# Second pair's xt copies behind its state products, and a state update moved to the third pair, in a retention and bilinear-MLP kernel

## The chip, the cores and the metric

The kernel runs on one core of a Trainium2 chip. The metric is the device time of one execution in microseconds (us); lower is better. The core's engines work side by side, each through its own list of instructions: TensorE (PE, with its weight loads shown apart as PEld), VectorE (DVE), ScalarE (ACT), GpSimd (POOL) and SyncE (SP), which issues the transfers. [...]

## What is computed

A retention recurrence over 4 batches, 8 heads, 768 positions and 64 features per head, followed by a bilinear MLP on the 3072 tokens:

```python
for t in range(S):
    state = gamma[None, :, None, None] * state + np.einsum('bhd,bhe->bhde', k[:, :, t], v[:, :, t])
    y[:, :, t] = scale * np.einsum('bhd,bhde->bhe', q[:, :, t], state)
...
x = attn_out.transpose(0, 2, 1, 3).reshape(B * S, H * D)
return ((x @ w_a) * (x @ w_b)) @ w_out
```

with w_a and w_b of 512x1536 and w_out of 1536x512. The output is float32; the kernel multiplies in bfloat16 and accumulates in float32.

## The kernel before

**The recurrence in chunks.** The decay is folded into tables that scale k and q, so that what is left is causal attention without a softmax. Tokens go in 24 slots of 128. Within a chunk of 64 positions the output is the masked score matrix times v (the intra products); what comes from earlier chunks is q times a running state (the state products), where the state is the sum of k times v over those chunks.

**The first batch** is worked in three pairs of slots (`PAIRS = 3`), u = 0, 1, 2, by functions whose names end in 2. A pair is loaded with even and odd positions in its two slots (par 0 and 1), and its chunks are its two halves c = 0 and 1. For each pair the code calls, by hand and in a chosen order:
- `casts2`: scales k and q and casts v, on the engines named;
- `flip2(u, K or Q, ...)`: transposes of k or q on PE, 128x128 each, and copies out of PSUM to kT2 or qT2 (`L397`);
- `scores2` and `mask2`: score products (`L410`) and the causal mask on DVE (`L421`);
- `intra2(u, par, begin, home)`: 16 intra products (`L466`) for one slot of the pair. They write y, which with `home` given is one PSUM tile whose two halves are `ys[u][0]` and `ys[u][1]`; so it is for u = 1;
- `inter2(u, last, cs)`: eight state products (`L451`) for each c named. Those of c take the state gbd[c], and add to the same y;
- `update2(u, c, on)`: 16 products of 64x64 (`L434`) that add chunk c of the pair to the state sum `st`, which stays in PSUM, then `keep_state(c, on)`, two casts of `st` into gbd[1 - c] on the engines in `on`; with `on=None` no casts;
- `leave2(u, on)`: casts y half by half into xt, the transposed activations that the MLP reads (`L182` on ACT, `L184` on DVE).

**The MLP** goes over token blocks `TILES = [4, 2, 2, 2, 2, 4, 4, 4]` in slots. For block J and one of 12 feature groups ft, `ffn_a` makes four products with w_a over the 512 input features (`L510`), which ACT casts to bfloat16 as asb (`L514`), and `ffn_g` four with w_b (`L522`), which DVE multiplies with asb into ht (`L525`). `ffn_out` makes the output products (`L550`). The results of `ffn_a` and `ffn_g` share three PSUM buffers, `ff`. The first block's first two groups are done by column halves: columns 0 to 255 (`0, W2`) are pair 0, columns 256 to 511 (`W2, 2 * W2`) are pair 1.

**What sets the order.** Every instruction passes through `seq`, which ties it to the one before it on its engine, so each engine runs in the order of the source. Waits between engines are put in from the tiles that are read and written. The weights are cast from float32 by POOL (`cast_w`), in the order in which their transfers land; `issue_loads(100)` puts the rest of the loads on SP's queue. After pair 1, 12 feature groups of block 0 run, and pair 2 is worked in among its last ones: `flip2(2, K)`, `ffn_a(0, 9)`, `flip2(2, Q)`, `ffn_g(0, 9)`, scores and masks, `update2(2, 0)` and so on. `flip2(2, K)` and the second half of `flip2(2, Q)` use the same PSUM bank, y0.

The part of the order that the change touches, before:

```python
    inter2(1, False, (0,))
    intra2(1, 1, False)
    leave2(1, (A_, None))
    W2 = 2 * P
    ffn_a(0, 0, 0, W2)
    inter2(1, True, (1,))
    leave2(1, (None, D_))
    ffn_a(0, 1, 0, W2)
    update2(1, 1, None)
```

Of the kernel before, what the change touches and what calls it, by code (L numbers as in the profile page):

```python
# [23 lines left out]
def kernel(  # L24
# [46 lines left out]
    def seq(bi):  # L71
        ins = bi.ins
        prev = last.get(ins.engine)
        if prev is not None:
            tc.add_manual_dep(ins, prev.name, nosync, reason="program order")
        last[ins.engine] = ins
        return bi
# [36 lines left out]
    def issue_loads(n):  # L114
        for _ in range(min(n, len(pending))):
            what = pending.pop(0)
            if what[0] in "kqv":
                load_pair(what[0], int(what[1:]))
            else:
                {"s": load_slot, "w": load_w, "o": load_o}[what[0]](int(what[1:]))  # L120
# [59 lines left out]
    def cast(engine, dst, src):  # L180
        if engine is nc.scalar:
            seq(nc.scalar.copy(dst, src))  # L182
        else:
            seq(engine.tensor_copy(dst, src))  # L184
# [50 lines left out]
    def half(i):  # L235
        return slice(64 * i, 64 * i + 64)
# [151 lines left out]
    def flip2(u, i, on, banks=None):  # L388
        into = (kT2, qT2)[i]
        if u not in into:  # L390
            into[u] = tra.tile([P, 2, HP, P], BF16, tag="kq"[i] + "T2", name="kq"[i] + "T2", bufs=2)
        for pars, eng in on:
            pool, tag = (psff, "ff") if not banks or not banks[pars[0]] else (psat, banks[pars[0]])
            tp = pool.tile([P, 2, HP, P], BF16, tag=tag, name="tp")[:, : len(pars)]
            for m, par in enumerate(pars):
                for hp in range(HP):
                    seq(nc.tensor.transpose(tp[:, m, hp, :], kqb[2 * u + par][:, i, hp, :, :], ident))  # L397
            cast(eng, into[u][:, pars[0] : pars[0] + len(pars)], tp)
# [25 lines left out]
    def update2(u, c, on=(nc.scalar, nc.scalar)):  # L424
        if (u, c) == (PAIRS - 1, 1):
            return
        if (u, c) == (0, 0):
            state[0] = psst.tile([P, HP, D], F32, tag="st", name="st")
        st = state[0]
        for par in range(2):  # L430
            for hp in range(HP):
                for r in range(2):
                    t = 2 * u + par
                    seq(nc.tensor.matmul(st[half(r), hp, :], kb[t][half(c), hp, r, :],  # L434
                                         vb[t][half(c), HP * r + hp, :],
                                         start=((u, c, hp, par) == (0, 0, 0, 0)),
                                         stop=(hp == HP - 1), skip_group_check=True))
        if on:
            keep_state(c, on)

    def keep_state(c, on=(nc.scalar, nc.scalar)):
        for r in range(2):
            cast(on[r], gbd[1 - c][half(r), :, half(r)], state[0][half(r), :, :])

    def inter2(u, last=False, cs=(0, 1)):
        for c in cs:
            if (u, c) == (0, 0):
                continue
            for r in range(2):
                for hp in range(HP):  # L450
                    seq(nc.tensor.matmul(ys[u][c][half(hp % 2), 2 * r + hp // 2, :],  # L451
                                         gbd[c][:, hp, half(r)],
                                         qT2[u][:, :, hp, half(c)], start=False, stop=last,
                                         skip_group_check=True))

    def intra2(u, par, begin, home=None):
        if begin and home is None:
            ys[u] = [psat.tile([P, HP, P], F32, tag=f"y{c}", name="y") for c in range(2)]
        elif begin:
            both = psat.tile([P, 2, HP, P], F32, tag=home, name="y")  # L460
            ys[u] = [both[:, c] for c in range(2)]
        t = 2 * u + par
        for r in range(2):
            for hp in range(HP):
                for c in range(2):
                    seq(nc.tensor.matmul(ys[u][c][half(hp % 2), 2 * r + hp // 2, :],  # L466
                                         vb[t][half(c), HP * r + hp, :], aT[t][half(c), r, hp, :],
                                         start=(begin and r == 0 and hp < 2), stop=not begin,
                                         skip_group_check=True))

    def leave2(u, on):
        J, i = where[2 * u]
        if i == 0 and J not in xt:
            xt[J] = xtp.tile([P, 4, KT, P], BF16, tag="xt", name="xt")
        for c, eng in enumerate(on):
            if eng is None:
                continue
            cast(eng, xt[J][:, i + c].rearrange("p k (m par) -> p k par m", par=2),
                 ys[u][c].rearrange("p k (par m) -> p k par m", par=2))

    def xcols(J, kt, c0, c1):
        if J < 2:
            return xt[J][:, c0 // P : c1 // P, kt, :]
        return xt[J][:, kt, c0:c1]
# [11 lines left out]
    def parts(J, ft, c0, c1):  # L496

        if J == 0 and ft in (2, 3):
            return [(c0, (c0 + c1) // 2), ((c0 + c1) // 2, c1)]
        return [(c0, c1)]  # L500

    def ffn_a(J, ft, c0=0, c1=None):
        c1 = TILES[J] * P if c1 is None else c1
        if J not in ht:
            ht[J] = htp.tile([P, NFT, 4 * P], BF16, tag="ht", name="ht")
        fs = slice(ft * P, (ft + 1) * P)
        a = psff.tile([P, 4 * P], F32, tag="ff", name="a")[:, : c1 - c0]
        for kt in range(KT):
            for b0, b1 in parts(J, ft, c0, c1):
                seq(nc.tensor.matmul(a[:, b0 - c0 : b1 - c0], wa_bf[:, kt, fs], xcols(J, kt, b0, b1),  # L510
                                     start=(kt == 0 and b0 == c0), stop=(kt == KT - 1 and b1 == c1),
                                     skip_group_check=True))
        asb = asbs[J, ft, c0] = asbp.tile([P, 4 * P], BF16, tag="asb", name="asb")[:, : c1 - c0]
        seq(nc.scalar.copy(asb, a))  # L514

    def ffn_g(J, ft, c0=0, c1=None):
        c1 = TILES[J] * P if c1 is None else c1
        fs = slice(ft * P, (ft + 1) * P)
        g = psff.tile([P, 4 * P], F32, tag="ff", name="g")[:, : c1 - c0]
        for kt in range(KT):  # L520
            for b0, b1 in parts(J, ft, c0, c1):
                seq(nc.tensor.matmul(g[:, b0 - c0 : b1 - c0], wb_bf[:, kt, fs], xcols(J, kt, b0, b1),  # L522
                                     start=(kt == 0 and b0 == c0), stop=(kt == KT - 1 and b1 == c1),
                                     skip_group_check=True))
        seq(nc.vector.tensor_tensor(ht[J][:, ft, c0:c1], g, asbs.pop((J, ft, c0)), op=ALU.mult))  # L525

    def ffn_ab(J, ft):
        store()
        ffn_a(J, ft)
        ffn_g(J, ft)  # L530
        catch_up(2)
# [30 lines left out]
    D_, G_, A_ = nc.vector, nc.gpsimd, nc.scalar  # L562
# [36 lines left out]
    intra2(1, 0, True, "at")  # L599
    update2(1, 0, (D_, D_))  # L600
    inter2(1, False, (0,))
    intra2(1, 1, False)
    leave2(1, (A_, None))
    W2 = 2 * P
    ffn_a(0, 0, 0, W2)
    inter2(1, True, (1,))
    leave2(1, (None, D_))
    ffn_a(0, 1, 0, W2)
    update2(1, 1, None)
    issue_loads(100)  # L610
    cast_w(1)
    ffn_g(0, 0, 0, W2)
# [2 lines left out]
    ffn_g(0, 1, 0, W2)  # L615
    ffn_g(0, 0, W2, 2 * W2)
    ffn_g(0, 1, W2, 2 * W2)
    keep_state(1)
    for ft in range(2, NFT):
        if ft % FPW == 0 and ft // FPW + 1 < NW - 1:  # L620
            cast_w(ft // FPW + 1)
# [8 lines left out]
        if ft == 8:  # L630
            ffn_ab(0, ft)
    flip2(2, K, [((0, 1), A_)], ("y0", None))
    ffn_a(0, 9)
    flip2(2, Q, [((0,), D_), ((1,), D_)], ("y1", "y0"))
    ffn_g(0, 9)
# [80 lines left out]
```

## Time and profile before

| | us |
|---|---|
| median of 3 runs | 225.2 (225.17 to 225.49) |
| the profiled execution | 225.04 |
| its span, first to last instruction | 223.3 |
| PE busy | 217.2 |
| DVE busy | 98.0 |
| ACT busy | 94.3 |
| POOL busy | 79.5 |

The profile is of one execution. Its timeline gives for each instruction, or for a run of like ones (xN), the start in us from the span's start, the length in us, the engine, the line, the operation and the tiles as out<-in; in brackets stands how long the engine was idle just before, and what ended that. Matmuls overlap in the pipeline, so the length of a group holds the time until its last result is written, while the next group starts earlier. Line numbers that start with L are those of the kernel before; a line such as L182 or L184 is a helper's that casts on ACT or on DVE and POOL.

### The profile page before, as it was taken

How to read it: one execution, taken by the hardware profiler on the slowest of the kernel's cores; microseconds unless marked ns; L12 is line 12 of the kernel's file. 1: busy time of each engine (PE TensorE's matmuls, PEld its weight loads, DVE VectorE, ACT ScalarE, POOL GpSimd, SP SyncE). 2: the span in 40 equal slices, each digit the busy share in tenths (PEclk: the TensorE clock that was granted, in tenths of full speed). 3: DMA queues.
4: the chain of work that ended last, by engine and by line, in shares of the span. 5: the costliest groups of instructions: out<-in, count | busy, mean ns of one | idle time of the engine just before them, and what ended most of it. 6: DMA issues, size and time to landing. Idle time of an engine off the chain costs nothing.

```text
span 223.3 us, 6286 instructions
## 1 busy us (share of the span) xinstructions
PE 217.2 (97%) x2633; PEld 131.4 (59%) x2633; DVE 98.0 (44%) x202; ACT 94.3 (42%) x202; POOL 79.5 (36%) x104
## 2 busy tenths in 40 slices
PE   7799999999999999999999999999999999999994
PEld 7568555785457866876875444554444544444443
DVE  3784446643316436572476333533333521333300
ACT  3784335343425425453456333455333354333221
POOL 5557798682634435351622535350000000000000
PEclk9999999999999999999999999999999999999999
DMA  6999999998999997999989497974100012100022
GB/s 179 346 379 382 366 292 396 300 217 178 221 244 230 256 219 101 229 203 231 236 181 222 96 268 190 248 127 144 47 0 0 3 50 94 47 3 0 3 94 94
DMA packets 96124, 39.72 MB, mean 178 GB/s; under 512 B 76000, under 2 KB 91616, under 8 KB 96096
## 3 DMA queue, kind: packets, MB, share of 16 engines
q1 hardware_dynamic: 95952, 39.20, 68.2%
q8 instruction: 20, 0.33, 0.6%
q10 hardware_dynamic: 144, 0.13, 0.2%
q14 instruction: 8, 0.07, 0.1%
HBM read 28.31 MB, written 6.29 MB: 155 GB/s over the span
## 4 chain that ended last, share of the span: by engine, by line
PE 93%; DMA 3%; POOL 1%; SPq 0%; ACT 0%; issue 0%; POOLq 0%
PE o L550 28%; PE g L522 28%; PE a L510 28%; DMA kf<-in_k_dram 3%; PE y L322 1%; POOL kqb L212 1%; PE y L334 1%; PE at L281 1%; PE st L257 1%; PE y L451 1%; PE st L434 1%; PE y L466 1%; PE tp L397 1%; PE at L410 0%; SPq L95 0%; ACT xt L182 0%
## 5 line engine op out<-in xcount | busy, mean ns | idle before, releaser
L525 DVE TENSOR_TENSOR ht<-g,asb 128x256 bf16<-128x256 f32 (+1 forms) x98 | 53.9, 550 | 82.3 <-PE g L522 73.8
L510 PE MATMUL a<-xt,wa_bf 128*128 128x256 bf16 (+1 forms) x400 | 77.7, 319 | 0.0
L522 PE MATMUL g<-xt,wb_bf 128*128 128x256 bf16 (+1 forms) x400 | 77.7, 319 | 0.0
L514 ACT CAST asb<-a 128x256 bf16<-128x256 f32 (+1 forms) x98 | 46.3, 472 | 71.8 <-PE a L510 71.8
L550 PE MATMUL o<-wo_bf,ht 128*128 128x512 bf16 (+2 forms) x312 | 64.5, 363 | 0.0
L510 PEld LDWEIGHTS <-wa_bf 128*128 128x128 bf16 x400 | 38.8, 98 | 23.9 <-DVE xt L184 0.4
L522 PEld LDWEIGHTS <-wb_bf 128*128 128x128 bf16 x400 | 38.9, 98 | 23.0
L550 PEld LDWEIGHTS <-ht 128*128 128x128 bf16 x312 | 28.8, 98 | 30.5
L212 POOL TENSOR_TENSOR kqb<-kf,ktab 128x512 bf16<-128x512 f32 x21 | 22.3, 1065 | 37.7 <-DMA kf<-in_k_dram 30.0
L182 ACT COPY osb<-o 128x512 f32<-128x512 f32 (+2 forms) x25 | 14.1, 564 | 36.3 <-PE o L550 29.9
L212 POOL TENSOR_TENSOR kqb<-qf,qtab 128x512 bf16<-128x512 f32 x21 | 22.3, 1063 | 2.4 <-DMA qf<-in_q_dram 2.3
L184 POOL CAST vb<-vf 128x512 bf16<-128x512 f32 x24 | 14.4, 610 | 20.8 <-DMA vf<-in_v_dram 15.1
L271 DVE TENSOR_TENSOR sums<-st,sums 128x256 f32<-128x256 f32 x30 | 12.7, 424 | 1.6
L182 ACT CAST gst<-sums 128x256 bf16<-128x256 f32 x26 | 10.4, 406 | 5.1 <-DVE sums L271 2.4
L287 DVE TENSOR_TENSOR aT<-at,mask 128x512 bf16<-128x512 f32 x18 | 11.5, 679 | 0.0
L345 ACT CAST xt<-y 128x512 bf16<-128x512 f32 x16 | 8.5, 584 | 0.7 <-PE y L334 0.7
L489 PE MATMUL idle<-zero 128*128 128x170 bf16 (+4 forms) x57 | 6.5, 275 | 1.3 <-DVE zero L126 1.3
L421 DVE TENSOR_TENSOR aT<-at,mask 128x512 bf16<-128x512 f32 x12 | 7.4, 682 | 0.2 <-PE at L410 0.2
L184 POOL CAST wa_bf<-wsta 128x1024 bf16<-128x1024 f32 (+1 forms) x7 | 6.4, 918 | 3.1 <-DMA wsta<-in_moe_w_a_dram 3.1
L184 POOL CAST wo_bf<-wsto 128x1024 bf16<-128x1024 f32 x6 | 6.2, 1040 | 2.8 <-DMA wsto<-in_moe_w_out_dram 2.8
L184 POOL CAST wb_bf<-wstb 128x1024 bf16<-128x1024 f32 (+1 forms) x7 | 6.4, 919 | 1.4 <-DMA wstb<-in_moe_w_b_dram 1.1
L299 DVE COPY lgr<-bq 128x1 f32<-128x1 f32 x4 | 0.6, 154 | 13.8 <-PE y L322 13.8
(56 smaller groups left out, 94.6 us busy)
## 6 DMA issues: line engine op xcount, KB each, us to landing
out_dram<-osb SPq DMA_DIRECT2D x23, 256.0 KB, 2.8
kf<-in_k_dram SPq DMA_DIRECT2D x18, 256.0 KB, 3.8
qf<-in_q_dram SPq DMA_DIRECT2D x18, 256.0 KB, 4.3
vf<-in_v_dram SPq DMA_DIRECT2D x18, 256.0 KB, 5.2
wsta<-in_moe_w_a_dram SPq DMA_DIRECT2D x6, 512.0 KB, 7.6
wstb<-in_moe_w_b_dram SPq DMA_DIRECT2D x6, 512.0 KB, 7.9
wsto<-in_moe_w_out_dram SPq DMA_DIRECT2D x6, 512.0 KB, 9.9
kf<-in_k_dram SPq DMA_DIRECT2D x3, 512.0 KB, 5.8
```

Source lines behind the costliest of these rows:

```text
L182: seq(nc.scalar.copy(dst, src))
L184: seq(engine.tensor_copy(dst, src))
L212: seq(eng.tensor_tensor(dst, src, tab, op=ALU.mult))
L271: seq(nc.vector.tensor_tensor(new, u[c][:, s], old, op=ALU.add))
L287: seq(nc.vector.tensor_tensor(aT[n][:, r].rearrange("p s h d -> p (s h) d"), at[:, r].rearrange("p s h d -> p (s h) d"), mask.to_broadcast ...
L345: seq(nc.scalar.copy(dst, ys[o][c]))
L421: seq(nc.vector.tensor_tensor(aT[t][:, r], ats[t][r], masks[par].to_broadcast([P, HP, P]), op=ALU.mult))
L510: seq(nc.tensor.matmul(a[:, b0 - c0 : b1 - c0], wa_bf[:, kt, fs], xcols(J, kt, b0, b1), start=(kt == 0 and b0 == c0), stop=(kt == KT - 1 a ...
L514: seq(nc.scalar.copy(asb, a))
L522: seq(nc.tensor.matmul(g[:, b0 - c0 : b1 - c0], wb_bf[:, kt, fs], xcols(J, kt, b0, b1), start=(kt == 0 and b0 == c0), stop=(kt == KT - 1 a ...
L525: seq(nc.vector.tensor_tensor(ht[J][:, ft, c0:c1], g, asbs.pop((J, ft, c0)), op=ALU.mult))
L550: seq(nc.tensor.matmul(o, ht[J][:, ft, i * P : (i + 1) * P], wo_bf[:, ft, c0:c1], start=(ft == 0), stop=(ft == NFT - 1)))
```

## The change

```diff
     intra2(1, 0, True, "at")
     update2(1, 0, (D_, D_))
     inter2(1, False, (0,))
-    intra2(1, 1, False)
-    leave2(1, (A_, None))
     W2 = 2 * P
     ffn_a(0, 0, 0, W2)
+    intra2(1, 1, False)
     inter2(1, True, (1,))
-    leave2(1, (None, D_))
+    leave2(1, (A_, D_))
     ffn_a(0, 1, 0, W2)
-    update2(1, 1, None)
     issue_loads(100)
     cast_w(1)
     ffn_g(0, 0, 0, W2)
...
     ffn_g(0, 1, W2, 2 * W2)
-    keep_state(1)
     for ft in range(2, NFT):
...
     flip2(2, K, [((0, 1), A_)], ("y0", None))
+    update2(1, 1)
     ffn_a(0, 9)
     flip2(2, Q, [((0,), D_), ((1,), D_)], ("y1", "y0"))
     ffn_g(0, 9)
```

Block a(0,0) on columns 0 to 255 now stands ahead of the second pair's last 16 intra products, not behind them. Both copies of the second pair's y into xt stand behind its last state products; before, ACT's copy of the first half stood ahead of a(0,0), and only DVE's behind. The state update of the second pair's second chunk, with its two casts on ACT, goes from the first block's early groups to behind the third pair's key transposes; before, its products and casts were apart. No instruction is added or left out.

## The prediction

> **What bounds the kernel now.** I read the page's busy shares, clock row and chain first, then the list of TensorE's waits, then the timeline around the edited lines.
>
> ```profile
> PE 217.2 (97%) x2633; PEld 131.4 (59%) x2633; DVE 98.0 (44%) x202; ACT 94.3 (42%) x202; POOL 79.5 (36%) x104
> ...
> PEclk9999999999999999999999999999999999999999
> ...
> PE 93%; DMA 3%; POOL 1%; SPq 0%; ACT 0%; issue 0%; POOLq 0%
> ```
>
> TensorE (PE) is busy 97% of the span at full granted clock and carries 93% of the chain that ended last. The question is whether it has slack anywhere, because without slack whatever delays it in one place reaches the end undiminished. The list of PE's waits, in us, times, longest:
>
> ```profile
> PE idle L489 <- DVE zero L126: 1.3, 1, 1.3
> PE tp L397 <- DVE kqb L212: 0.7, 4, 0.2
> PE tp L397 <- POOL kqb L212: 0.5, 1, 0.5
> PE y L451 <- ACT xt L182: 0.3, 1, 0.3
> ```
>
> The first three belong to the warm-up and the first transposes, all before the edit. The fourth is the stall that the change is about. After it PE waits for no other engine by this list, so I take both differences below as passing 1:1 to the end.
>
> The first stretch, in the timeline (start, length, instruction; the bracket is idle time before it and what ended it):
>
> ```profile
> 14.78 0.61 POOL L184 CAST wa_bf<-wsta 128x512 bf16<-128x512 f32 x1 [1.27 <-DMA wsta<-in_moe_w_a_dram]
> ...
> 14.85 0.41 PE L451 MATMUL y<-qT,gbd 128*64 128x128 bf16 x8
> ...
> 15.02 0.87 DVE L184 CAST gbd<-st 64x256 bf16<-64x256 f32 x2
> ...
> 15.20 0.42 PE L466 MATMUL y<-aT,vb 64*64 64x128 bf16 x16
> 15.54 0.33 PEld L510 LDWEIGHTS <-wa_bf 128*128 128x128 bf16 x4
> 15.55 0.61 PE L510 MATMUL a<-xt,wa_bf 128*128 128x256 bf16 x4
> 15.67 0.73 ACT L182 CAST xt<-y 128x512 bf16<-128x512 f32 x1 [0.47 <-PE y L466]
> ...
> 16.45 0.41 PE L451 MATMUL y<-qT,gbd 128*64 128x128 bf16 x8 [0.29 <-ACT xt L182]
> ...
> 16.80 0.61 PE L510 MATMUL a<-xt,wa_bf 128*128 128x256 bf16 x4
> 16.97 0.73 DVE L184 CAST xt<-y 128x512 bf16<-128x512 f32 x1 [1.08 <-PE y L451]
> 17.34 0.33 PEld L434 LDWEIGHTS <-kqb 64*64 64x64 bf16 x16 [0.21 <-issue]
> 17.34 0.44 PE L434 MATMUL st<-vb,kqb 64*64 64x64 bf16 x16
> ...
> 17.71 0.61 PE L522 MATMUL g<-xt,wb_bf 128*128 128x256 bf16 x4
> ...
> 18.15 1.04 PE L510 MATMUL a<-xt,wa_bf 128*128 128x256 bf16 x8
> ```
>
> Matmuls are pipelined, so I price a group by the distance from its start to the next group's start, not by its length. That gives 0.44 for four 128x256 products (17.71 to 18.15), 0.35 for the 16 last intra products (15.20 to 15.55), 0.35 for eight state products (16.45 to 16.80) and 0.37 for the 16 products of a state update (17.34 to 17.71). From the full-array products at 16.80 to the 64x64 products at 17.34 it is 0.54, that is 0.44 and 0.10 for the switch.
>
> What should be seen is who guards the pair's output. The state products of 16.45 write the second half of it, and yet they waited until ScalarE (ACT) had copied the first half (15.67+0.73=16.40, start 16.45). Both halves lie in one PSUM tile, and the tile is guarded as a whole.
>
> **The change, part one: the last copies.** Nothing is added; four groups change places. In the built program the order on PE becomes: state products c=0, block a(0,0), 16 intra products, state products c=1, a(0,1), g(0,0), then the second-half block a. On ACT the c=0 copy now stands behind the cast of a(0,0) and in front of that of a(0,1). Its wait counts through the last c=1 state product, and VectorE's (DVE) c=1 copy waits on ACT's semaphore at the very count that ACT's c=0 copy raises. The old program has a wait on ACT there too, but the copy that it names had ended 0.57 before DVE began (16.40 against 16.97). So the two copies, 0.73 each, which before were far apart, now stand one behind the other, both behind the last state product. The removed stall is real, but the first reader of both copies, the second-half block a, is only two blocks further down.
>
> Step by step, in us of the old timeline, with 0.05 for a hand-over (16.40 to 16.45):
> - State products c=0 leave PE free at 15.20. Block a(0,0) now needs the first weight cast at once, which ends on POOL at 14.78+0.61=15.39. It starts at 15.45. Before, 0.35 of intra products covered this; now PE idles 0.25.
> - Four products to 15.89, switch 0.10, intra 0.35 to 16.34, state products c=1 0.35 to 16.69. Their operand from DVE was there at 15.89 (15.02+0.87), so nothing waits. The old place was 16.80: the gain so far is 0.11, not 0.29, since the cover of a(0,0) is paid back.
> - The last state product ends 0.06 after the issue stops (16.45+0.41=16.86 against 16.80), so at 16.75. ACT copies 16.80 to 17.53. For ACT waking DVE I take 0.08, between 0.05 and the 0.11 of PE waking DVE (16.86 to 16.97). DVE copies 17.61 to 18.34, and the second-half a starts at 18.39.
> - PE, meanwhile, does a(0,1) and g(0,0) to 16.69+0.88=17.57 and then idles 0.82. Before, the state update stood there and used 0.47 of this time.
>
> The second-half a starts at 18.39 instead of 18.15: **+0.24**. Three hand-overs between 0.05 and 0.11 and a weight transfer that lands a little later or earlier give bounds of +0.10 and +0.45. ACT's cast of a(0,1), pushed behind the copy, ends near 17.96 (17.53+0.05+0.38 by the row below) and is needed at 18.83, one block after 18.39. DVE's first gated product moves from 18.43 to about 18.39, so it delays nobody.
>
> ```profile
> 16.26 0.38 ACT L514 CAST asb<-a 128x256 bf16<-128x256 f32 x1
> ...
> 18.43 0.42 DVE L525 TENSOR_TENSOR ht<-g,asb 128x256 bf16<-128x256 f32 x1 [0.72 <-PE g L522]
> ```
>
> **Part two: the moved state update.** Its 16 products and ACT's two casts go behind the third pair's key transposes. No DMA moves with them, and the SP and POOL queues keep their order.
>
> ```profile
> 32.46 0.61 PE L397 MATMUL tp<-ident,kqb 128*128 128x128 bf16 x8
> ...
> 32.91 1.03 PE L510 MATMUL a<-xt,wa_bf 128*128 128x512 bf16 x4
> 33.11 1.01 ACT L182 COPY kT<-tp 128x1024 bf16<-128x1024 bf16 x1 [0.72 <-PE tp L397]
> ...
> 33.77 0.78 PE L397 MATMUL tp<-ident,kqb 128*128 128x128 bf16 x8
> ...
> 34.02 0.59 ACT L514 CAST asb<-a 128x512 bf16<-128x512 f32 x1
> 34.17 0.38 PE L397 MATMUL tp<-ident,kqb 128*128 128x128 bf16 x4
> 34.40 1.03 PE L522 MATMUL g<-xt,wb_bf 128*128 128x512 bf16 x4
> 35.35 0.64 PE L410 MATMUL at<-qT,kT 64*64 64x128 bf16 x32
> 35.53 0.69 DVE L525 TENSOR_TENSOR ht<-g,asb 128x512 bf16<-128x512 f32 x1 [0.51 <-PE g L522]
> ```
>
> On PE it costs 0.37 and a switch of 0.10, since full-array transposes stand ahead of it now: 0.47. Against it stands a small stall of the old order that the wait list doesn't name. Eight transposes take 0.45 (32.46 to 32.91), so the four of 33.77 are issued by 34.00, but the next four begin at 34.17, after the key copy ended (33.11+1.01=34.12): they write the bank that it reads. With the update in front of them they come 0.47 later and don't wait: 0.17 is returned. Part two is **+0.30**. Bounds: +0.10, if the update hides the rest of its time in some other short wait, and +0.47 without any cover.
>
> ACT's two casts cost nothing as long as this holds: the old pair of them took 0.74, so the cast of block 9 goes from 34.02 to about 34.76 and ends at 35.35. The score products that reuse its buffer come at 35.35+0.30=35.65, and DVE's product at 35.53+0.30=35.83. The margin is 0.30; beyond it these would be late.
>
> ```profile
> 19.50 0.74 ACT L182 CAST gbd<-st 64x256 bf16<-64x256 f32 x2
> ```
>
> The sum is +0.24 and +0.30, so +0.54 on the profiled execution of 225.04 (span 223.3): 225.58. The three runs shown have a median of 225.2, 0.16 above that execution, which puts the forecast at 225.74; I say **225.7**. Own range of this case: +0.20 to +0.92, 225.4 to 226.1.
>
> **Rivals.**
>
> *The copies run side by side (not slower).* If DVE's copy doesn't wait for ACT's, it ends at 16.75+0.11+0.73=17.59, the second-half a starts at 17.64, and part one becomes -0.51. With part two the sum is -0.21: 225.0; at the lower bound of part two -0.41: 224.8. It decides in DVE's copy alone. For it speaks that the third pair does just that, with the two halves in tiles of their own:
>
> ```profile
> 39.98 0.73 ACT L182 CAST xt<-y 128x512 bf16<-128x512 f32 x1 [1.20 <-PE y L451]
> ...
> 40.20 0.73 DVE L184 CAST xt<-y 128x512 bf16<-128x512 f32 x1 [0.38 <-PE y L451]
> ```
>
> Against it: the second pair has one tile for both, whose whole-tile guard cost 0.29 at 16.45, and the new wait list names ACT's copy. [...]
>
> *ACT becomes late behind the third pair (slower).* The key copy (1.01), the two moved casts (0.74) and the cast of block 9 (0.59) now follow one another on ACT within one block's time. If this runs more than the margin of 0.30 late, the second score matrix, DVE's product and the next block wait. Its price is at most the two casts' 0.74 less the margin, 0.44: 226.2. Against it: ACT is idle 0.72 ahead of the key copy.
>
> *The stall was worth its 0.29 and the update is free.* Then the time is 225.2-0.29=224.9. Against it is the start of the second-half a at 18.15 itself, which did not wait before and has two copies in front of it now.
>
> **How the numbers follow.** The forecast's case gets 0.75, side by side 0.10, ACT late 0.11, the stall as a plain gain 0.04. The range runs from 225.1, which takes in the upper part of the side-by-side case, to 226.1. About 0.2%, 0.45 us, is what a measurement of this kernel can tell from no change, so slower means above 225.65 and faster below 224.75. The forecast lies just above that line; its unknowns, hand-overs and lost cover, mostly add, so I give three quarters of its case to slower: 0.75 x 0.75 + 0.11 = 0.67. Faster takes half of the side-by-side case and half of the last one, which both end near that line: 0.07. The rest, 0.26, is no change.
>
> **What would show it.** Right: an ACT copy of xt near 16.8, DVE's beginning as it ends, a PE wait of about 0.8 for DVE's xt at the block a near 18.4, and the idle of 0.25 for POOL's wa_bf at 15.45. Behind the key transposes, 16 st products with a switch ahead, no pause between the two query groups, and the scores 0.5 later than 35.35. Wrong: copies that overlap, a second-half a before 18.15, or scores waiting for ACT's asb.

## The result, and the profile after

| | before | changed kernel |
|---|---|---|
| median of 21 runs each, us | 225.25 (225.01 to 225.78) | 225.84 (225.59 to 226.56) |
| ratio | | 1.0024, 95% interval 1.0012 to 1.0035 |
| the profiled execution, us | 225.04 | 225.95 |
| its span, us | 223.3 | 224.2 |

The change costs 0.59 by the medians. The two profiled executions lie 0.91 apart, because before's lies 0.21 below its median and the changed kernel's 0.11 above. So 0.59 is the price, with an interval of 0.27 to 0.79 by the ratio, and the traces say where such time goes. Of the runs reported further down two, 231.6 and 232.28 us of two kernels with a finer warm-up, lie 2.0 and 1.9% above the fastest run of their kernels at a granted clock of 0.993, count as slow and are left out of the medians.

The page of the changed kernel, its lines on busy time and on the chain that ended last:

```profile
PE 215.7 (96%) x2613; PEld 132.0 (59%) x2633; DVE 97.6 (44%) x202; ACT 94.3 (42%) x202; POOL 79.4 (35%) x104
...
PE 90%; DMA 3%; SPq 3%; issue 1%; ACT 0%; DVE 0%; POOL 0%
```

TensorE (PE) carries 90% of the chain instead of 93%. Its list of waits, in us, times, longest:

```profile
PE idle L489 <- DVE zero L126: 1.3, 1, 1.3
PE o L550 <- issue: 1.1, 7, 0.2
PE a L510 <- DVE xt L184: 0.6, 1, 0.6
PE tp L397 <- POOL kqb L212: 0.5, 1, 0.5
PE a L510 <- POOL wa_bf L184: 0.4, 1, 0.4
PE y L451 <- issue: 0.3, 1, 0.3
```

The line of 1.1 at the output products is none of the change's. The page's costliest groups have only 299 of these products:

```profile
L550 PE MATMUL o<-wo_bf,ht 128*128 128x512 bf16 (+2 forms) x299 | 62.5, 362 | 1.4 <-issue 1.1
```

There are 312 weight loads for them, and 312 products in before's trace: 13 records are missing, and the holes look like pauses of 0.16. The same goes for PE's busy time, 215.7 against 217.2, with 2613 products beside 2633 loads. Such a line is read against the counts first.

The wait for ScalarE's (ACT) xt is gone. In its place stand two: block a waits for VectorE's (DVE) xt, and block a(0,0) waits for the weight cast on GpSimd (POOL). The timeline shows where:

```profile
14.91 0.41 PE L451 MATMUL y<-qT,gbd 128*64 128x128 bf16 x8
...
15.10 1.17 POOL L184 CAST wa_bf<-wsta 128x512 bf16<-128x512 f32 x2 [1.49 <-DMA wsta<-in_moe_w_a_dram]
...
15.77 0.61 PE L510 MATMUL a<-xt,wa_bf 128*128 128x256 bf16 x4 [0.44 <-POOL wa_bf L184]
...
16.31 0.42 PE L466 MATMUL y<-aT,vb 64*64 64x128 bf16 x16
...
16.66 0.41 PE L451 MATMUL y<-qT,gbd 128*64 128x128 bf16 x8
...
17.00 0.61 PE L510 MATMUL a<-xt,wa_bf 128*128 128x256 bf16 x4
17.11 0.74 ACT L182 CAST xt<-y 128x512 bf16<-128x512 f32 x1 [0.32 <-PE y L451]
...
17.45 0.60 PE L522 MATMUL g<-xt,wb_bf 128*128 128x256 bf16 x4
...
17.88 0.73 DVE L184 CAST xt<-y 128x512 bf16<-128x512 f32 x1 [1.93 <-ACT xt L182]
...
18.67 1.03 PE L510 MATMUL a<-xt,wa_bf 128*128 128x256 bf16 x8 [0.62 <-DVE xt L184]
```

ACT's copy ends at 17.11+0.74=17.85 and DVE's begins at 17.88, with ACT's xt as its releaser. PE issues the last g(0,0) product at 17.90 (17.45 and 0.45 for four products), and then stands until 18.67. In what follows, "the stretch" is the distance from the start of the second pair's c=0 state products to the start of the second-half block a. It was 18.15-14.85=3.30 before and is 18.67-14.91=3.76 now: +0.46.

The chain, in order of time (start, us, what), shows what ends last there:

```profile
7.76 7.29 DMA wsta<-in_moe_w_a_dram
...
15.10 0.62 POOL wa_bf L184
...
15.77 0.61 PE a L510 x4
...
17.11 0.75 ACT xt L182
...
17.88 0.74 DVE xt L184
...
18.67 1.03 PE a L510 x8
```

It goes back from the block to both copies in a row, and further to the landing of a weight transfer. The transfer had 0.35 of intra products as cover before; now whatever it is late reaches the second-half block a.

The third pair, in the timeline:

```profile
32.98 0.61 PE L397 MATMUL tp<-ident,kqb 128*128 128x128 bf16 x8
33.52 0.44 PE L434 MATMUL st<-vb,kqb 64*64 64x64 bf16 x16
33.89 1.04 PE L510 MATMUL a<-xt,wa_bf 128*128 128x512 bf16 x4
34.76 0.61 PE L397 MATMUL tp<-ident,kqb 128*128 128x128 bf16 x8
35.21 1.03 PE L522 MATMUL g<-xt,wb_bf 128*128 128x512 bf16 x4
36.17 0.64 PE L410 MATMUL at<-qT,kT 64*64 64x128 bf16 x32
...
37.09 1.24 PE L510 MATMUL a<-xt,wa_bf 128*128 128x512 bf16 x5
```

The eight query transposes of 34.76 now run in one piece of 0.61, where they took 0.78 with a pause in them. From the key transposes to the scores it is 36.17-32.98=3.19; before it was 35.35-32.46=2.89. That is +0.30.

The books balance: the stretch starts 0.06 later, grows by 0.46, and the third pair by 0.30. Block 10's a comes 0.82 later (37.09; before, 36.27 by the timeline). The last 0.08 of the 0.90 between the spans comes after 98 us.

### The profile page after: what moved, and what is told of

Its sections match the earlier page's. It is cut to its first block, busy times and chain, and to the rows that moved or that the text cites. A ratio compares the mean times of both kernels' runs of the same rounds, so it can differ in the third digit from the quotient of the medians.

```text
span 224.2 us, 6264 instructions
## 1 busy us (share of the span) xinstructions
PE 215.7 (96%) x2613; PEld 132.0 (59%) x2633; DVE 97.6 (44%) x202; ACT 94.3 (42%) x202; POOL 79.4 (35%) x104
## 4 chain that ended last, share of the span: by engine, by line
PE 90%; DMA 3%; SPq 3%; issue 1%; ACT 0%; DVE 0%; POOL 0%
PE a L510 28%; PE g L522 28%; PE o L550 28%; DMA wsta<-in_moe_w_a_dram 3%; SPq L95 3%; PE y L322 1%; PE at L281 1%; PE y L334 1%; PE st L257 1%; PE y L451 0%; PE y L466 0%; PE tp L397 0%; ACT xt L182 0%; DVE xt L184 0%; POOL wa_bf L184 0%
## 5 line engine op out<-in xcount | busy, mean ns | idle before, releaser
L550 PE MATMUL o<-wo_bf,ht 128*128 128x512 bf16 (+2 forms) x299 | 62.5, 362 | 1.4 <-issue 1.1
```

The costliest lines, as they stand in the source:

```text
L550: seq(nc.tensor.matmul(o, ht[J][:, ft, i * P : (i + 1) * P], wo_bf[:, ft, c0:c1], start=(ft == 0), stop=(ft == NFT - 1)))
```

## The experiments

Each kernel was run beside the kernel before in the same session (its medians were 225.12 to 225.19), and differences are against that; the changed kernel's 225.84 is from another session. "Late" is the distance from the start of the last g before the third pair's key transposes to its scores: 3.75 before (31.60 to 35.35), 4.05 in the changed kernel (32.12 to 36.17).

### Each part by itself

**The update's move alone**, in the kernel before:

```diff
-    update2(1, 1, None)
...
-    keep_state(1)
...
     flip2(2, K, [((0, 1), A_)], ("y0", None))
+    update2(1, 1)
```

> The kernel before with only the state update and its two casts moved behind the third pair's key transposes. My account: the early place gives back 0.40 (the block g at 17.71 comes at 17.24, and the second-half block a then has to wait for DVE's xt copy, 17.70 + 0.05 = 17.75 instead of 18.15), and the late place costs 0.30, so about 0.1 below the kernel before, 225.15 against 225.25; flip K to the scores takes 3.19 as in the changed kernel. Rival, that the moved update is the whole loss of 0.59: 225.8.

225.21 against 225.13, ratio 0.9998 (0.9986 to 1.0009). The timeline, in the stretch that starts at 15.44 here:

```profile
17.39 0.61 PE L510 MATMUL a<-xt,wa_bf 128*128 128x256 bf16 x4
17.84 0.60 PE L522 MATMUL g<-xt,wb_bf 128*128 128x256 bf16 x4
18.36 1.05 PE L510 MATMUL a<-xt,wa_bf 128*128 128x256 bf16 x8
```

g(0,0) follows a(0,1) after 0.45 instead of 0.91, and the stretch falls to 18.36-15.44=2.92, 0.38 less than before. Late rises by 0.30, to 4.05. In the old order the update was work on the path in both places, so its move is nearly free: 0.08 less by the trace, and nothing that the medians can tell from no change. The rival, that it is the whole loss, is out.

**The copies alone**: the changed kernel with the update back at its early place.

```diff
     ffn_a(0, 1, 0, W2)
+    update2(1, 1, None)
...
+    keep_state(1)
...
-    update2(1, 1)
```

> The changed kernel with the state update left at its early place, its casts behind the block's first groups as before. My account: both copies still one behind the other ahead of the second-half block a, the update fills 0.47 of PE's wait there and costs nothing, and nothing is paid at the third pair: about +0.29 on the kernel before, 225.5, with PE's wait for DVE's xt near 0.2 to 0.35. Rival, that the update's move is the whole loss: 225.25. Rival, that the idle wait itself is a cost beside the update: 225.8 as the changed kernel.

225.56 against 225.13, +0.43, ratio 1.0021 (1.0013 to 1.003).

```profile
17.00 0.61 PE L510 MATMUL a<-xt,wa_bf 128*128 128x256 bf16 x4
17.54 0.44 PE L434 MATMUL st<-vb,kqb 64*64 64x64 bf16 x16
17.91 0.61 PE L522 MATMUL g<-xt,wb_bf 128*128 128x256 bf16 x4
18.67 1.03 PE L510 MATMUL a<-xt,wa_bf 128*128 128x256 bf16 x8
```

The update fills part of the time in which PE stands for the copies, and the second-half a starts no earlier for its absence: the stretch is 18.67-14.92=3.75 with it and 3.76 without. Late is 3.75, without the price. So by the traces the two parts are bound to each other: once the copies leave PE a hole, the update's old place costs nothing, and moving it away buys nothing and pays 0.30 at the third pair. The medians are too coarse to show it: the parts by themselves cost 0.08 and 0.43, and together 0.59.

### Who serialises the copies

**The changed kernel with a tile for each half**, everywhere that the two-bank tile `at` was used:

```diff
-            both = psat.tile([P, 2, HP, P], F32, tag=home, name="y")
-            ys[u] = [both[:, c] for c in range(2)]
+            ys[u] = [psat.tile([P, HP, P], F32, tag=f"{home}{c}", name="y") for c in range(2)]
```

> The changed kernel with the two-bank PSUM tile of the second pair's output split into two tiles of a bank each (its tag is split in all its uses, scores too). My account: DVE's copy no longer waits for ACT's, both start within 0.1 of each other, the second-half block a starts 0.75 earlier, and the time falls from 225.84 to about 225.1, below the kernel before. Rival, that the late weight cast ahead of block a(0,0) is the cost and the order of the copies is covered: no more than 0.1 below 225.84.

226.03 against 225.13, ratio 1.0036 (1.0018 to 1.0054): the time is a miss. Locally the timeline does what was expected:

```profile
16.83 0.74 ACT L182 CAST xt<-y 128x512 bf16<-128x512 f32 x1
...
17.18 0.74 DVE L184 CAST xt<-y 128x512 bf16<-128x512 f32 x1 [0.95 <-PE y L451]
...
17.97 1.05 PE L510 MATMUL a<-xt,wa_bf 128*128 128x256 bf16 x8
```

The copies overlap, DVE's releaser is PE, and the stretch is 17.97-15.19=2.78, 0.98 shorter. Of that, 0.22 is a weight cast that came earlier against PE in this execution. The gain was lost far away: this kernel's list of waits holds a new one, near 118 us, and DVE pauses at 109.

```profile
PE y L322 <- DVE gst L184: 0.5, 1, 0.5
```

The split changed the buffers of every later scores tile too. The three kernels further down with the old warm-up, in which the second pair's output alone is split, have the pause at 109 but not this wait, so the wait comes with the rest of the split.

**The kernel before with the same split** does the same:

> The kernel before with the same tile split in two. My account: the state products of the second half wait no more for ACT's copy but only for the state's cast and the switch (start 16.10 instead of 16.45), so about 0.35 below the kernel before, 224.9. Rival, that this stall is covered by what comes later (the transfers of the weights): within 0.1 of 225.25.

225.71 against 225.13, ratio 1.002 (1.0006 to 1.0034). The stretch is 18.39-15.45=2.94, 0.36 below before's and as expected; but PE loses 0.24 at 109 us and some 0.4 near 118, and the time is a miss.

**Banks of their own for the second pair's output alone**, all other uses as they were. This is the edit of the next three kernels, and of one further down:

```diff
-            ys[u] = [both[:, c] for c in range(2)]
+            ys[u] = [psat.tile([P, HP, P], F32, tag="y0", name="y"), both[:, 0]]
```

In the changed kernel:

> The changed kernel with the second pair's output in banks of their own. My account: the two copies overlap, the second-half block a comes 0.7 earlier, none of the later losses of the run that split the tile everywhere: 225.1 to 225.2 against 225.84. Rival, that the weight cast ahead of block a(0,0) holds the stretch: no more than 0.2 below the changed kernel.

225.36 against 225.19, ratio 0.9998 (0.9984 to 1.0012): 0.48 below the changed kernel's 225.84.

```profile
14.94 0.41 PE L451 MATMUL y<-qT,gbd 128*64 128x128 bf16 x8
...
15.41 0.61 PE L510 MATMUL a<-xt,wa_bf 128*128 128x256 bf16 x4
...
16.41 0.74 ACT L182 CAST xt<-y 128x512 bf16<-128x512 f32 x1
16.76 0.74 DVE L184 CAST xt<-y 128x512 bf16<-128x512 f32 x1 [0.76 <-PE y L451]
...
17.56 1.05 PE L510 MATMUL a<-xt,wa_bf 128*128 128x256 bf16 x8
```

The order of the work is the changed kernel's; only the tiles differ, and the copies no longer stand in a row. The stretch is 17.56-14.94=2.62, 1.14 less than the changed kernel's. Of that, 0.39 is a weight cast that came earlier against PE (15.41-14.94=0.47, where the changed kernel had 0.86), and 0.75 is the copies'. This settles that the tile's guard makes the two copies wait for each other.

In the kernel before:

> The kernel before, with only the second pair's output in two tiles: the first half in the free bank y0, the second in one bank of the old tile, and no other use of that tile changed. My account: as in the run with the tile split everywhere, the second half's state products start 0.35 earlier, with none of that run's later losses at 110 and 118 us: 0.35 below the kernel before, near 224.8. Rival, that some later wait takes this gain back: within 0.1 of the kernel before.

225.11 against 225.12, ratio 0.9993 (0.9983 to 1.0004), a miss: the rival's case. The wait of 0.29 is gone: from a(0,0) to the state products it is 16.33-15.79=0.54 instead of 0.90. But a(0,0) waited for its weights here, 15.79-14.92=0.87 behind the c=0 state products instead of 0.70, and took 0.17 back. And DVE pauses later:

```profile
109.22 0.93 DVE L525 TENSOR_TENSOR ht<-g,asb 128x256 bf16<-128x256 f32 x2 [0.82 <-PE a L510]
```

Two gated products stand together after an idle time of 0.82, where before each had 0.45 ahead of it; PE's blocks come 0.24 later from there on. This pause is in each of the six kernels with banks of their own, at 108.9 to 110.2 us, and not in the kernels without. What causes it is open.

In the kernel before, with the update moved as well:

> The kernel before with the second pair's output in banks of their own, and the state update moved behind the third pair's key transposes. My account: the stretch to the second-half block a is 0.75 shorter (0.35 for the stall, 0.40 for the update that no longer stands there), and the third pair pays 0.30: 0.45 below the kernel before, near 224.7. Rival, that the early place of the update was idle time anyway: 0.05 below the kernel before.

224.98 against 225.12, ratio 0.9989 (0.9979 to 1.0000). A miss: 0.45 was expected. The stretch is 17.41-14.92=2.49, 0.81 below before's; 0.30 of it goes to the third pair, 0.23 to DVE's pause, and some 0.1 is lost near 118 us. In the end the profiled execution, 224.90, is 0.14 below before's, and so is the median. It is the fastest kernel of the study, and not clearly below before.

### What covers the weights, and where the update goes

**Block a(0,0) behind the intra products again**, in the changed kernel:

```diff
-    ffn_a(0, 0, 0, W2)
     intra2(1, 1, False)
+    ffn_a(0, 0, 0, W2)
```

> The changed kernel with block a(0,0) behind the 16 intra products again; both copies stay behind the last state products and the update stays at the third pair. My account: the weight cast, which kept PE waiting 0.44 in the changed kernel's profile, has 0.35 of cover again, so the second-half block a starts 0.1 to 0.3 earlier; 225.5 to 225.7 against 225.84, still above the kernel before, since the two copies are still one behind the other. Rival, that the two copies in a row alone are the loss of part one and the weight cast is hidden: 225.84.

225.62 against 225.12, ratio 1.0019 (1.0007 to 1.0031), as expected: 0.22 below the changed kernel.

```profile
15.72 0.41 PE L451 MATMUL y<-qT,gbd 128*64 128x128 bf16 x8
...
18.18 0.73 DVE L184 CAST xt<-y 128x512 bf16<-128x512 f32 x1 [1.42 <-ACT xt L182]
...
18.96 1.03 PE L510 MATMUL a<-xt,wa_bf 128*128 128x256 bf16 x8 [0.61 <-DVE xt L184]
```

The wait for POOL is gone, the copies still stand in a row, and the stretch is 18.96-15.72=3.24, 0.06 below before's. So by this trace the copies in a row cost no more than the stall and the update that they took the place of, and the cost of part one is the cover that a(0,0) lost. What stays is the third pair's 0.30 (Late is 36.45-32.40=4.05) less the 0.06, that is 0.24; by the medians it is 0.50, with an interval of 0.16 to 0.70. The opposite kernel, with a(0,0) moved ahead and ACT's copy left in its early place, wasn't run.

**The update ahead of the key transposes**, in the changed kernel:

```diff
+    update2(1, 1)
     flip2(2, K, [((0, 1), A_)], ("y0", None))
-    update2(1, 1)
```

> The changed kernel with the moved state update ahead of the third pair's key transposes instead of behind them. My account: the pause of 0.18 between the two groups of query transposes comes back, because the key copy is no longer covered, so from the end of the block ahead to the scores it takes 0.17 to 0.18 more than in the changed kernel; the time is 226.0 against 225.84. Rival, that the copy is no cover and the order doesn't matter: 225.84, no pause.

226.25 against 225.12, ratio 1.004 (1.0026 to 1.0055), 0.41 above the changed kernel where 0.17 was expected. Late is 36.44-32.00=4.44, 0.39 more than the changed kernel's.

```profile
33.43 0.74 ACT L182 CAST gbd<-st 64x256 bf16<-64x256 f32 x2 [0.65 <-PE st L434]
34.20 1.01 ACT L182 COPY kT<-tp 128x1024 bf16<-128x1024 bf16 x1
...
34.65 0.39 PE L397 MATMUL tp<-ident,kqb 128*128 128x128 bf16 x4
...
35.27 0.38 PE L397 MATMUL tp<-ident,kqb 128*128 128x128 bf16 x4 [0.23 <-ACT kT L182]
```

The two casts now stand ahead of the key copy on ACT, which pushes the copy back. Between the two groups of query transposes PE loses 35.27-34.65-0.22=0.40 instead of 0.17. What the expectation lacked is that an update takes its casts along.

### The pause at the state products of the first pair

In the profiles so far PE paused between the sixth or seventh and the last of the first pair's state products, near 13.6 us, with no releaser, and for 0.14 to 1.26 us by the weight-load rows. In these rows it is always the same load that comes late, the program's 225th. As the start of the stretch hangs on it, it was moved by lengthening the warm-up, with as many columns in all (36 x 170 and 60 x 102 are both 6120) but 24 products more:

```diff
-warm(36, psat, "y1", 170)
+warm(60, psat, "y1", 102)
```

In the kernel before:

> The kernel before with its first warm-up products cut finer: 60 of 102 columns instead of 36 of 170, the same columns in all, so that 24 more pairs of PE instructions stand ahead of everything else. The question is the pause without a releaser inside the state products at 13.6, which lasted 0.2 to 1.1 in the profiles so far and always ended at the same product. Theory that PE there runs out of instructions, whose transfer (16 KB, 11.6 to 12.5 in the traces) lands about 2.3 after it starts: the pause moves 24 products ahead, where PE arrives with more time, and shrinks to under 0.2; the median falls by 0.1 to 0.4 and the runs scatter less. Rival, that the pause belongs to the work there (the state's cast): it stays at the seventh state product, and the median stays within 0.1 of the kernel before.

228.57 (227.75 to 230.38) against 225.19, ratio 1.0143 (1.011 to 1.0175): a miss in the time by 3.4. The pause itself did what the theory said: it stood ahead of the last of the 16 score products instead of the last of the eight state products, 1+16+7=24 products earlier and so again ahead of the 225th weight load, and it was short, 0.18. What the theory lacked are the new pauses, in the timeline's weight loads:

```profile
13.40 0.10 PEld L410 LDWEIGHTS <-kT 64*64 64x64 bf16 x1 [0.18 <-issue]
...
20.29 0.99 PEld L522 LDWEIGHTS <-wb_bf 128*128 128x128 bf16 x10 [0.91 <-issue]
...
123.92 0.98 PEld L550 LDWEIGHTS <-ht 128*128 128x128 bf16 x6 [2.42 <-issue]
```

Counted at the same weight load in both kernels, PE falls behind before by 0.80 at the pause of 20.3 us, 0.36 near 99, 0.57 near 118 and 2.30 at that of 123.9. That is 4.03 of the 5.4 by which the span of this execution, the longest of its six, exceeds before's (228.7 against 223.3). Of the rest, 0.9 comes behind the last weight load; it wasn't traced.

With banks of their own and the update moved:

> The kernel before with the second pair's output in banks of their own, the state update moved to the third pair, and the finer warm-up. If the gains add: the 0.14 that the first two brought, and what the finer warm-up brings alone, so 224.6 to 224.9. Rival, that an earlier arrival only turns into a wait for the weight cast of block a(0,0): 225.0, with PE waiting for POOL's wa_bf.

227.58 (227.12 to 230.42) against 225.19, ratio 1.0114 (1.007 to 1.0159), a miss for the same reason: counted in the same way, PE loses 1.08 near 99 us, 0.34 near 118 and 0.94 near 122.

In the changed kernel:

> The changed kernel with the finer warm-up. In the changed kernel PE waits for the first weight cast anyway behind the pause, so a shorter pause should be worth less than in the kernel before: the median falls by 0 to 0.15, and the gap between the two kernels with the finer warm-up is 0.6 to 0.9. Rival, that the pause weighs the same in both: the gap stays 0.6.

228.89 (227.91 to 229.98) against 225.19, ratio 1.0136 (1.0106 to 1.0165), where a little less than 225.84 was expected. It is 0.32 above the kernel before with the same warm-up, where 0.6 to 0.9 was expected; with a scatter of 2.6 and 2.1 us, this decides nothing.

## Why the prediction was right, and where a term was off

**The sum** was +0.54, and the medians differ by 0.59. The shift of 0.16 from the profiled execution to the median of before was the right step too: it is 0.21 with the 21 runs. That +0.54 and +0.59 lie so close is in part luck: between the two traces the parts are +0.46 and +0.30, and the 0.59 has an interval of half a microsecond.

**The copies in a row** were as forecast. The releaser is ACT's xt, the hand-over took 0.03 instead of 0.08, and PE stood for 0.77 (17.90 to 18.67) instead of 0.82. From a(0,0) to the second-half a the forecast was 18.39-15.45=2.94, and 2.90 was measured. That the tile's guard does it was an inference from the old wait, and the kernels with banks of their own show it.

**The idle time for the weights** is the term that was mis-sized. The forecast had 0.25 of it, from POOL's cast at 14.78 in one execution. In the changed kernel's profile the cast began at 15.10 and a(0,0) stood 15.77-14.91=0.86 behind the state products, that is 0.51 beyond their own 0.35. In the four other profiles with this order and the old warm-up the same figure is 0.49, 0.29, 0.27 and 0.12. So 0.25 is within what occurs, but it is no constant: it varies by 0.4 from one profile to another, and one profile gives one draw. The mean of the five is 0.34. The other terms of part one nearly cancel, in the forecast (+0.24 with 0.25 of idle time) as in the traces (3.24 against 3.30 with a(0,0) put back), so its size is that of this idle time. The kernel before hides the first 0.35 of it behind the intra products. The bounds of +0.10 to +0.45 for part one, set for three hand-overs and the transfer, were used up by the weights alone: +0.46 in the trace, and +0.43 by the medians of the copies alone, whose interval (+0.29 to +0.68, from its ratio) leaves +0.24 out.

**The update's price** was forecast at 0.37 and 0.10 less 0.17. The trace shows +0.30 to the hundredth, with the pause between the query transposes gone as its cover was to show. In medians it is 0.59 less 0.43, 0.16, from two sessions, so no finer than some tenths.

**ACT behind the third pair** did not become late: the cast of block 9 began at 35.30 and the scores did not wait for it. The margin of 0.30 held. ACT did hold PE up where the casts stand ahead of the key copy, in the kernel with the update ahead of the keys (a wait of 0.23 for ACT's kT, Late 4.44 against 4.05).

**Side by side** did not come about in the one tile, as argued: DVE's copy has ACT's xt as its releaser and began at 17.88, 0.03 behind the end of ACT's. In the changed kernel with banks of their own the two copies overlap: ACT's lasts from 16.41 to 17.15 (16.41+0.74), and DVE's begins at 16.76 with PE as its releaser. What the forecast of 225.0 for that case lacked is the rest of the way to the end. With the copies overlapping, the changed kernel stood at 225.36, 0.48 lower: of the copies' 0.75, DVE's pause at 109 us took 0.25 back.

**The stall as a plain gain** is out: the wait for ACT at 16.45 is gone, and its 0.29 came back at the next reader of the same tile.

## What to carry to other kernels

Before a stall is removed by moving work, ask who reads the late result next and what covered the work that moves up: here the copies' first common reader was two blocks on, and a weight cast lost its 0.35 of cover. A filler moved out of a place costs twice if the same change turns that place into idle time (here the stretch was 3.75 with the update and 3.76 without, and the third pair paid 0.30), so cost the parts together as well as apart. The tile of both halves was guarded as one (DVE's copy began 0.03 behind the end of ACT's); splitting it made two copies overlap, but of a gain of 0.75 us at 18 us into the run a third was lost at 109 us, so the end has to be measured too.

## What the runs showed of the hardware

**PE's pauses without a releaser stood at fixed places in the count of its weight loads.** Twenty-four products more at the start, with as many columns, cost 3.4 us (228.57 against 225.19), in pauses up to 2.42 us at other places (the weight-load rows, which have no records missing). The first pause stands ahead of the 225th weight load with either warm-up, be it one of the state products or of the score products. The long ones with the finer warm-up stand ahead of the 352nd, 1375th, 1631st and 1759th: 127, 1023, 256 and 128 loads apart, multiples of 128 within one. The page of the changed kernel has a queue that fits:

```profile
q8 instruction: 20, 0.33, 0.6%
```

Its 20 packets are of 16384 bytes each in the traces of the changed kernel and of the kernel before, and their kind is instruction. The traces hold each packet's times, and they fit a late transfer: in the kernel before a packet ended at 12.44 and PE went on at 13.87, in the changed kernel 12.91 and 14.14, so PE went on 1.43 and 1.23 us behind the packet's end. It is the first packet of the queue in both. Counted on from the 225th weight load in steps of 128, to the 2529th, each of these 19 loads begins behind the end of the packet of the same rank, by 1.23 us at the least over both traces. No run moved a packet alone: that its arrival ends the pause is argued from these times, and not shown by an experiment.

**The weight transfer's landing varied by as much as the effects at issue**: in the profiles with the old warm-up POOL's cast began between 14.74 and 15.29, 0.55 apart, where the medians differ by 0.59. How much of a kernel's scatter (225.59 to 226.56 for the changed one) is due to this and how much to the pauses wasn't separated.
